# Filling TensorE's planned gaps with constant matmuls before the feed-forward part, and a plan in which the loads begin later

## The chip, the cores and the metric

The kernel runs on one core of one Trainium2 chip. The metric is the device time of one execution in microseconds; less is better. Three runs of the kernel before gave 295.18, 295.59 and 295.64 us, a median of 295.59 us.

## The reference

Two stages, one after the other, on 8 batches of 8 heads, 576 positions and head size 64. First a Nyströmformer attention, with 32 landmarks a head:

```python
q_lm = q.reshape(B, H, m, S // m, D).mean(axis=3)       # m = 32 landmarks
k_lm = k.reshape(B, H, m, S // m, D).mean(axis=3)
A = sm(q, k_lm); Bm = sm(q_lm, k_lm); C = sm(q_lm, k)    # scaled softmaxes
Z = Bm.T / (norm1(Bm) * norminf(Bm) + 1e-6)
for _ in range(6):
    Z = 2 * Z - Z @ Bm @ Z
attn = A @ Z @ C @ v
```

Then a feed-forward part on the 4608 positions of width 512, with a hidden width of 2048:

```python
h = attn_as_rows @ w_in            # 4608 x 512 @ 512 x 2048
g = maximum(h, 0) ** 2
out = g @ w_out                    # 4608 x 2048 @ 2048 x 512, float32
```

## The kernel before

All inputs come in float32 and are turned into bf16 by the loading DMAs, which GpSimd (POOL) issues: one for the k, q and v of each batch (`kb`, `qb`, `vb`), four for `w_in`, four for `w_out`. An issue waits until the load eight places earlier has landed (`LOADS = 8`). Stores go out from SP.

For each batch, `attention(b)` makes: the landmark means of k and q (`means`, into `mps`, matmuls with the constant `seg`, L334), scaled by `part` and turned by `folded` into the landmarks `lm` (L356); transposes of k and q on TensorE (`tps`, L458), evacuated to `kT` and `qT`; the small scores (`scores_b`, L379), whose normalised result is `bn`, with its column sums (`sums_b`, L406); the scores of q's landmarks against k (`scores_c`, `cps`, L490) with their maximum `nmc` and exponential `ec`; six steps of the iteration (`start_r` for `rps`, then `product` for `ips`, both L572, each followed by an update of `st` on VectorE); the transposes of `ec` (`turn_c`, `ctp`, L530) and the product with v (`times_v`, `ups`, L543), giving `u`; the scores of q (`scores_a`, `aps`, L700), for the first batch with the shift added by a matmul with `ident` (`shift_a`, L727); and the transposes of the normalised q scores (`transpose_a`, `atp`, L770) into `AT`. `times_z` (L631) gives `wT`, and `times_w_in` (L649) multiplies it with `w_in` into `G`, so that the first feed-forward matmul is G times AT.

The feed-forward part takes the positions in 9 stretches of 512. `ff_first` makes one 128x512 block of the hidden layer in the PSUM tag "h" (two buffers; `hps`, two matmuls or more, L848), ScalarE takes the relu (L855), VectorE the square (L860). `ff_second` makes 128 rows of the output from 16 matmuls (`ops`, L879).

The order of the instructions on each engine is made by the planner `Order`. Every step is added with an engine (or a choice of engines), a cost in us, the keys it reads and writes, and an urgency. `run` keeps in `free` the time at which each engine is through with what it was given, and in `end` the time at which each step ends. Again and again it works out for every step that could go next when it could start: not before its engine is free, not before its inputs' ends plus a latency (0.25 us after TensorE, 2.2 us after a DMA, 0.1 us else), and not before a PSUM slot is free. It takes the one that can start first, then the more urgent. Steps of batch 0 are kept by the length of the chain behind them. The step's `emit` is called at once, so instructions stand on every engine in the order in which the planner took them. No planned time is written into the program; engines run as soon as their semaphores allow. In this planner's terms a load is an issue of 0.8 us on POOL and a transfer of 3.05 us (k, q, v) or 2.5 us (weights).

Of the kernel before, what the change touches and what calls it, by code (L numbers as in the profile page):

```python
# [8 lines left out]
P = 128  # L9
# [5 lines left out]
BF16 = mybir.dt.bfloat16  # L15
F32 = mybir.dt.float32
# [14 lines left out]
SB = 512  # L31
# [28 lines left out]
class Order:  # L60
# [3 lines left out]

    BIAS = {"DVE": 0.6}
    LATENCY = {"PE": 0.25, "DMA": 2.2, "XBAR": 0.1, "SP": 2.5}

    def __init__(self, psum):  # L70
        self.slots = {tag: [0.0] * n for tag, n in psum.items()}
        self.tasks, self.writers, self.readers, self.taker = [], {}, {}, {}
        self.first, self.firsts = False, []

    def add(self, engine, cost, emit, reads=(), writes=(), urgency=0, takes=None, gives=None,
            reuses=()):

        i = len(self.tasks)
        deps = set()
        for key in list(reads) + list(writes):  # L80
            deps.update(self.writers.get(key, ()))
        for key in reuses:
            old = self.readers.get(key, []) + self.writers.get(key, [])
            deps.update(old)
            if gives is not None:

                self.tasks[self.taker[gives]][3].update(old)
        for key in reads:
            self.readers.setdefault(key, []).append(i)
        for key in writes:  # L90
            self.writers.setdefault(key, []).append(i)
        if takes:
            self.taker[takes[2]] = i
        self.tasks.append((engine, cost, emit, deps, urgency, takes, gives))
        if self.first:
            self.firsts.append(i)
        return i
# [30 lines left out]
        return seen  # L128

    def run(self):  # L130
        free, end, ran, held, left = {}, {}, {}, {}, list(range(len(self.tasks)))
        order, tail = [], self.tails()
        while left:
            best, other = None, None
            soon = self.coming(end, ran, free) if any(i not in end for i in self.firsts) else {}
            for i in left:
                choice, cost, _, deps, urgency, takes, _ = self.tasks[i]
                if any(d not in end for d in deps):
                    continue
                options = []  # L140
                for engine, cost in choice.items() if cost is None else ((choice, cost),):
                    start = free.get(engine, 0.0)
                    for d in deps:
                        start = max(start, end[d] + (self.LATENCY.get(ran[d], 0.1)
                                                     if ran[d] != engine else 0.0))
                    if takes:
                        at = sorted(self.slots[takes[0]])[:takes[1]]
                        if len(at) < takes[1]:
                            continue
                        start = max(start, at[-1])  # L150
                    options.append((start + cost + self.BIAS.get(engine, 0.0), start, engine, cost))
                for _, start, engine, cost in sorted(options)[:1]:
                    this = (start, urgency - tail.get(i, 0.0), i, cost, engine)
                    if other is None or this < other:
                        other = this
                    mine = tail.get(i, 0.0)
                    if any(e == engine and j != i and
                           max(at + tail[j], (at + c + mine) if mine else 0.0)
                           < max(max(at, start + cost) + tail[j], start + mine) - 0.05
                           for j, (e, at, c) in soon.items()):  # L160
                        continue
                    if best is None or this < best:
                        best = this
            start, _, i, cost, engine = best or other
            choice, fixed, emit, _, _, takes, gives = self.tasks[i]
            ran[i] = engine
            end[i] = free[engine] = start + cost
            if takes:
                slots = self.slots[takes[0]]
                slots.sort()  # L170
                del slots[:takes[1]]
                held[takes[2]] = [takes[0], takes[1], takes[3], 0.0]
            if gives is not None:
                h = held[gives]
                h[2] -= 1
                h[3] = max(h[3], end[i] + 0.1)
                if h[2] == 0:
                    self.slots[h[0]] += [h[3]] * h[1]
            left.remove(i)
            order.append((start, i))  # L180
            if emit is not None:
                if fixed is None:
                    emit(engine)
                else:
                    emit()
        self.ran = ran
        return order, end
# [3 lines left out]
def kernel(  # L191
# [9 lines left out]
    nc = tc.nc  # L201

    const = ctx.enter_context(tc.tile_pool(name="const", bufs=1))
# [4 lines left out]
    psum = ctx.enter_context(tc.tile_pool(name="psum", bufs=1, space=bass.MemoryType.PSUM))  # L208
# [9 lines left out]
    od = Order({"at": 2, "n": 1, "h": 2, "o": 1})  # L218
# [19 lines left out]
    def load(src, name, b, bufs):  # L238
        def go():
            t = T[name, b] = qkv.tile([TP, H, J * D], BF16, tag=name, bufs=bufs,  # L240
                                      name=f"{name}{b}")
            nc.gpsimd.dma_start(t[:], src[b].rearrange("h (p j) d -> p h (j d)", j=J))  # L242
        add_load(3.05, go, (name, b), -200 + b, [(name, b - bufs)])
# [20 lines left out]
    seg = const.tile([TP, M], BF16, name="seg")  # L264
    ones = const.tile([P, M], F32, name="ones")
    mask = const.tile([P, NPAIR], F32, name="mask")


    fold = const.tile([P, 3, P], BF16, name="fold")
# [12 lines left out]
                                compare_op=ALU.is_ge, fill=0.0, base=M - 1, channel_multiplier=-1)  # L282

    def fills():
        nc.vector.memset(seg_f[:], 1.0)
        nc.vector.memset(ones[:], 1.0)
        nc.vector.memset(mask[:], 1.0)
# [4 lines left out]
    def make_fold():  # L292
        nc.vector.memset(fold[:, 0:2], 0.0)
        for i in range(2):
# [3 lines left out]
                                    in0=fold[:, i, 64 * i:64 * i + 64], scalar1=0.125,  # L298
                                    scalar2=None, op0=ALU.mult)

    od.add("DVE", 1.0, fills, writes=["fills"], urgency=-20)
    load(k, "kb", 0, 2)
    load(q, "qb", 0, 2)
# [531 lines left out]
    def ff_first(s, f, at):  # L835
        segs, n = [], s * SB
        while n < (s + 1) * SB:
            b = n // S
            e = min((s + 1) * SB, (b + 1) * S)
            segs.append((b, n - b * S, e - b * S, n - s * SB))  # L840
            n = e
        box = {}

        def product():
            box["h"] = hps = psum.tile([P, SB], F32, tag="h", bufs=2, name=f"hps{s}")
            for b, lo, hi, o in segs:
                for g in range(2):
                    nc.tensor.matmul(hps[:, o:o + hi - lo],  # L848
                                     lhsT=T["G", b][:, g, P * f:P * f + P],
                                     rhs=T["AT", b][:, g, lo:hi],  # L850
                                     start=(g == 0), stop=(g == 1))

        def relu():
            box["r"] = r = moep.tile([P, SB], BF16, tag="r", bufs=5, name=f"r{s}")
            nc.scalar.activation(r[:], box["h"][:], AF.Relu)  # L855

        def square():
            if f == 0:
                T["gT", s] = moep.tile([P, NF, SB], BF16, tag="gT", name=f"gT{s}")
            nc.vector.tensor_tensor(T["gT", s][:, f, :], box["r"][:], box["r"][:], ALU.mult)  # L860

        u = at
        od.add("PE", 0.45, product, [key for b, lo, hi, _ in segs
                               for key in [("G", b, f // 4, 0), ("G", b, f // 4, 1)]
                               + [("AT", b, 0)] * (lo < 512) + [("AT", b, 1)] * (hi > 512)],
               [("hp", s, f)], u, takes=("h", 1, ("hps", s, f), 1))
        od.add("ACT", 0.6, relu, [("hp", s, f)], [("r", s * NF + f)], u, gives=("hps", s, f),
               reuses=[("r", s * NF + f - 5)])
        od.add("DVE", 0.45, square, [("r", s * NF + f)], [("gT", s, f)], u,
               reuses=[("gT", s - 2, i) for i in range(NF)])  # L870
# [37 lines left out]
    def feed(s):  # L908

        for i in range(NF):  # L910
            if s < N_SB:
                ff_first(s, i, 100 * s + 3 * i)
            if s:
                ff_second(s - 1, i // 4, 4 * (i % 4), 100 * s + 3 * i + 2)
# [44 lines left out]
```

## Time and profile before

| | |
|---|---|
| median of 3 runs | 295.59 us |
| the profiled execution's own time | 295.65 us |
| its span, first to last instruction | 293.9 us |
| TensorE (PE) busy | 268.2 us, 91% |
| weight loads (PEld) busy | 147.9 us |
| ScalarE (ACT) / VectorE (DVE) / GpSimd (POOL) busy | 180.7 / 171.5 / 28.1 us |
| mean granted TensorE clock | 0.985 |
| first PE instruction with data | 7.43 us |
| first `hps` matmul (L848) | 32.77 us |

The profile gives, for each engine, the time in which it ran an instruction, the granted TensorE clock as a share of full speed, the idle time before an instruction and what ended it ("issue" where the profile shows nothing that it waited for), and the chain of waits that ended last.

### The profile page before, as it was taken

Reading aid. Unit: us, or ns where it says so; the run is one execution under the profiler, and the core shown is the slowest. Engines: PE = TensorE matmul, PEld = TensorE weight load, DVE = VectorE, ACT = ScalarE, POOL = GpSimd, SP = SyncE. Lnnn points to the kernel's source line nnn. Section 1 sums busy time; section 2 is a strip of 40 time slices with the busy share of each in tenths; the row PEclk is TensorE's granted clock in tenths of the full one; section 3 lists DMA queues with packets and bytes.
Section 4 is the critical chain, followed back from the end, with each engine's and each line's share of the span. In section 5 each row is a group of like instructions: output and inputs, shape, how many; then the busy total and the mean of one; then the engine's idle time right before and its main releaser. Section 6 shows DMA issues by size and latency. Waiting matters only on the chain.

```text
span 293.9 us, 8012 instructions
## 1 busy us (share of the span) xinstructions
PE 268.2 (91%) x3357; PEld 147.9 (50%) x3403; DVE 171.5 (58%) x435; ACT 180.7 (61%) x334; POOL 28.1 (10%) x43
## 2 busy tenths in 40 slices
PE   0966889899999999999999999999999999999993
PEld 0744544555455555555656654565554444444441
DVE  1178499678849954986598368847775333323100
ACT  1447689676787847684777485566667745556220
POOL 8523212210030003000300000000000000000000
PEclk9999599999999999999999999999999999999998
DMA  7999999999999985992799201111111112211222
GB/s 97 204 205 207 205 206 203 204 218 129 186 165 217 162 167 79 216 197 59 112 198 175 52 21 37 39 38 38 36 39 38 45 49 53 71 38 38 67 74 71
DMA packets 52452, 34.20 MB, mean 116 GB/s; under 512 B 25280, under 2 KB 47808, under 8 KB 52416
## 3 DMA queue, kind: packets, MB, share of 16 engines
q0 software_dynamic: 23040, 18.35, 41.3%
q1 hardware_dynamic: 29376, 15.34, 26.4%
q8 instruction: 26, 0.43, 0.6%
q14 instruction: 10, 0.08, 0.1%
HBM read 36.70 MB, written 9.44 MB: 157 GB/s over the span
## 4 chain that ended last, share of the span: by engine, by line
PE 78%; DVE 9%; DMA 4%; ACT 3%; issue 3%; SPq 1%; POOL 0%; POOLq 0%
PE ops L879 38%; PE hps L848 21%; PE mps L334 3%; DMA qb<-in_q_dram 3%; PE gps L649 3%; PE ips L572 2%; PE ctp L530 2%; PE aps L700 2%; DVE G L224 2%; DMA out_dram<-o 1%; DVE gT L860 1%; PE atp L770 1%; ACT G L222 1%; DVE rsa L746 1%; PE cps L490 1%
## 5 line engine op out<-in xcount | busy, mean ns | idle before, releaser
L879 PE MATMUL ops<-w_out,gT 128*128 128x512 bf16 x534 | 137.9, 379 | 2.9 <-issue 1.1
L855 ACT ACTIVATE r<-hps 128x512 bf16<-128x512 f32 x144 | 83.2, 601 | 50.2 <-PE hps L848 47.4
L860 DVE TENSOR_TENSOR gT<-r 128x512 bf16<-128x512 bf16 x144 | 59.1, 428 | 44.9 <-ACT r L855 43.9
L848 PE MATMUL hps<-AT,G 128*128 128x512 bf16 (+7 forms) x508 | 82.7, 288 | 0.9 <-ACT r L855 0.3
L879 PEld LDWEIGHTS <-gT 128*128 128x128 bf16 x576 | 52.0, 98 | 50.2 <-issue 2.2
L848 PEld LDWEIGHTS <-G 128*128 128x128 bf16 x512 | 40.6, 98 | 27.7 <-issue 4.3
L224 DVE CAST G<-gps 128x512 bf16<-128x512 f32 x25 | 16.6, 688 | 22.3 <-ACT G L222 22.2
L222 ACT COPY o<-ops 128x512 f32<-128x512 f32 x31 | 18.2, 586 | 17.2 <-PE ops L879 11.2
L222 ACT CAST G<-gps 128x512 bf16<-128x512 f32 x39 | 21.3, 593 | 3.7 <-PE gps L649 3.2
L607 DVE SCALAR_TENSOR_TENSOR st<-st,ips 128x128 bf16<-128x128 bf16 x40 | 11.2, 280 | 7.6 <-PE ips L572 7.3
L507 ACT ACTIVATE ec<-cps,nmc 128x576 bf16<-128x576 f32 x16 | 11.7, 740 | 4.2 <-DVE nmc L498 4.2
L572 PEld LDWEIGHTS <-st 32*32 32x32 bf16 x384 | 5.6, 90 | 17.0 <-issue 5.0
L242 POOL DMA_DIRECT2D kb<-in_k_dram x8 | 6.4, 797 | 81.4 <-PE mps L334 76.5
L649 PE MATMUL gps<-w_in,wT 64*32 64x512 bf16 x256 | 12.5, 404 | 0.9 <-ACT wT L222 0.4
L572 PE MATMUL ips<-st 32*32 32x64 bf16 (+1 forms) x384 | 11.5, 194 | 1.9 <-DVE st L581 1.3
L334 PE MATMUL mps<-seg,kb 96*128 96x32 bf16 x192 | 6.1, 178 | 7.4 <-DMA kb<-in_k_dram 7.4
L222 ACT COPY ct<-ctp 96x1536 bf16<-96x1536 bf16 x7 | 10.0, 1435 | 3.8 <-PE ctp L530 3.7
L498 DVE TENSOR_REDUCE nmc<-cps 128x1 f32<-128x576 f32 x16 | 11.6, 750 | 0.8 <-PE cps L490 0.7
L746 DVE TENSOR_REDUCE rsa<-ea 128x36 f32<-128x1152 f32 (+2 forms) x10 | 11.1, 1106 | 0.4 <-ACT ea L736 0.2
L222 ACT COPY kT<-tps 128x1152 bf16<-128x1152 bf16 x6 | 6.7, 1128 | 7.5 <-PE tps L458 7.5
L712 DVE TENSOR_REDUCE ma<-aps 128x32 f32<-128x1024 f32 (+1 forms) x9 | 9.9, 1098 | 1.8 <-PE aps L700 1.1
L222 ACT COPY AT<-atp 128x1024 bf16<-128x1024 bf16 (+1 forms) x8 | 7.7, 959 | 4.5 <-PE atp L770 4.2
(89 smaller groups left out, 236.1 us busy)
## 6 DMA issues: line engine op xcount, KB each, us to landing
out_dram<-o SPq DMA_DIRECT2D x40, 128.0 KB, 2.4
kb<-in_k_dram POOLq DMA_DIRECT2D x8, 576.0 KB, 10.5
qb<-in_q_dram POOLq DMA_DIRECT2D x8, 576.0 KB, 13.2
vb<-in_v_dram POOLq DMA_DIRECT2D x8, 576.0 KB, 14.8
out_dram<-o SPq DMA_DIRECT2D x40, 64.0 KB, 1.9
w_in<-in_moe_w_in_dram POOLq DMA_DIRECT2D x4, 512.0 KB, 18.4
w_out<-in_moe_w_out_dram POOLq DMA_DIRECT2D x4, 512.0 KB, 21.0
out_dram<-o SPq DMA_DIRECT2D x8, 192.0 KB, 2.2
```

The costliest lines, as they stand in the source:

```text
L222: nc.scalar.copy(dst, src)
L224: nc.vector.tensor_copy(dst, src)
L334: nc.tensor.matmul(X["mps"][:, ti, h, :], lhsT=T[name, b][:, h, P * c:P * c + P], rhs=seg[:], start=(c == 0), stop=(c == 2))
L498: nc.vector.reduce_max(X["nmc"][:, g:g + 1], X["cps"][g][:, :, 0:HALF], axis=AX.XY, negate=True)
L507: nc.scalar.activation(X["ec"][:, g, :].rearrange("p (f n) -> p f n", f=2), X["cps"][g][:, :, 0:HALF], AF.Exp, bias=X["nmc"][:, g:g + 1], ...
L572: nc.tensor.matmul(out(r, g), lhsT=lhsT(r, g), rhs=rhs(r, g), start=True, stop=True)
L649: nc.tensor.matmul(gps[M * p:M * p + M, g, :], lhsT=X["wT"][r, p, :], rhs=w_in_bf[c][r, p, :], start=True, stop=True)
L746: nc.vector.reduce_sum(X["rsa"][:, r], X["ea"][:, r], axis=AX.X)
L848: nc.tensor.matmul(hps[:, o:o + hi - lo], lhsT=T["G", b][:, g, P * f:P * f + P], rhs=T["AT", b][:, g, lo:hi], start=(g == 0), stop=(g == 1))
L855: nc.scalar.activation(r[:], box["h"][:], AF.Relu)
L860: nc.vector.tensor_tensor(T["gT", s][:, f, :], box["r"][:], box["r"][:], ALU.mult)
L879: nc.tensor.matmul(T["o", s, ts][:], lhsT=T["gT", s][:, f, P * ts:P * ts + P], rhs=w_out_bf[f // 4][:, f % 4, :], start=(f == 0), stop=(f ...
```

## The change

Three things are added; nothing is taken away.

First, the planner starts with POOL free at 1.4 us instead of 0, so in the plan the loads begin 1.4 us later.

Second, DVE's first instruction becomes a memset of a 128x512 bf16 tile `plain` with ones, ahead of the three memsets that it did before.

Third, while the planner takes steps, up to the first `ff_first` product, it looks before each TensorE step at the planned idle time of TensorE in front of it. If that is over 0.3 us, `filler` is called first. It puts matmuls of `plain` with itself onto TensorE's queue, 512 columns at most each, down to 64, into a tile `dummy` that takes one of the two buffers of tag "h" and that nothing reads. The first call gives (gap - 1.0) x 1200 columns, each later one (gap - 0.2) x 2400, gap in us.

```diff
+    START = 1.4
     BIAS = {"DVE": 0.6}
...
+        self.filler, self.fill_until = None, None
...
-        free, end, ran, held, left = {}, {}, {}, {}, list(range(len(self.tasks)))
+        free, end, ran, held, left = {"POOL": self.START}, {}, {}, {}, list(range(len(self.tasks)))
...
             choice, fixed, emit, _, _, takes, gives = self.tasks[i]
+            if i == self.fill_until:
+                self.filler = None
+            if engine == "PE" and self.filler and start - free.get("PE", 0.0) > 0.3:
+                self.filler(start - free.get("PE", 0.0))
...
+    plain = const.tile([P, SB], BF16, name="plain")
...
     def fills():
+        nc.vector.memset(plain[:], 1.0)
         nc.vector.memset(seg_f[:], 1.0)
...
+    box = {}
+
+    def filler(time):
+        if "dummy" not in box:
+            box["dummy"] = psum.tile([P, SB], F32, tag="h", bufs=2, name="dummy")
+            columns = int((time - 1.0) * 1200)
+        else:
+            columns = int((time - 0.2) * 2400)
+        while columns >= 64:
+            n = min(columns, SB)
+            nc.tensor.matmul(box["dummy"][:, 0:n], lhsT=plain[:, 0:P], rhs=plain[:, 0:n],
+                             start=True, stop=True)
+            columns -= n
+
+    od.filler = filler
...
-        od.add("PE", 0.45, product, [key for b, lo, hi, _ in segs
+        ff = od.add("PE", 0.45, product, [key for b, lo, hi, _ in segs
...
+        if od.fill_until is None:
+            od.fill_until = ff
```

## The prediction

> **What bounds the kernel now.** I read the page's head and busy slices first, then the windows, then the start by the timeline, the chain of waits and POOL's rows, because every added matmul lies ahead of the first `hps` at 32.77 us.
>
> ```profile
> span 293.9 us, 8012 instructions
> PE   0966889899999999999999999999999999999993
> PEclk9999599999999999999999999999999999999998
> ```
>
> ```profile
> 30.00:32.00 2.00, 1.74 (x21) 1.07 (x17) 1.02 (x2) 0.72 (x2) 0.77 (x1) 0.50 1.30 203
> 40.00:50.00 10.00, 9.32 (x163) 5.12 (x166) 9.55 (x23) 9.59 (x17) 0.69 (x1) 1.00 1.30 204
> 150.00:200.00 50.00, 48.93 (x695) 28.52 (x704) 34.45 (x87) 33.56 (x63) 0.00 (x0) 1.00 0.36 70
> ```
>
> A window's columns are length, busy time of PE, PEld, DVE, ACT and POOL, granted clock, DMA share, GB/s. From 75 us on PE is full; from 40 to 50 us DVE and ACT are nearly full too. Whatever brings the start forward moves all this forward unchanged, so a microsecond won before the first `hps` should be one at the end. Loads keep the DMA queues at some 205 GB/s for the first 50 us and could cap that.
>
> ```profile
> 7.43 0.82 PE L334 MATMUL mps<-seg,kb 96*128 96x32 bf16 x24 [7.43 <-DMA kb<-in_k_dram]
> 8.09 2.08 PE L458 MATMUL tps<-ident,kb 96*128 96x96 bf16 x24
> ...
> 21.81 0.61 PE L727 MATMUL aps<-ma,ident 128*128 128x512 bf16 x1
> ...
> 23.21 0.38 PE L727 MATMUL aps<-ma,ident 128*128 128x512 bf16 x1 [0.56 <-DVE ma L712]
> ...
> 24.32 1.20 PE L458 MATMUL tps<-ident,kb 96*128 96x96 bf16 x24
> ...
> 29.57 0.48 PE L334 MATMUL mps<-seg,qb 96*128 96x32 bf16 x12 [1.39 <-issue]
> ...
> 34.47 1.04 PE L848 MATMUL hps<-AT,G 128*128 128x512 bf16 x2
> ```
>
> The same 24 transposes take 2.08 us at 8.09 and 1.20 at 24.32, the same L727 matmul 0.61 and 0.38. So PE runs at half rate until about 22.5 us, although the clock column says 1.00 there (nothing was recorded before the first change). It runs at full rate until 29.3 us and again at 0.50 until 36.1. PE was 95% busy from 7.4 to 14.0 without winning the clock: with transposes and 32-column matmuls. From 32.77 on, with 512-column ones, it won it in 3.4 us. That is the case for wide filler.
>
> **The plan.** Adding the planner's own costs: the first load is issued by 0.8 and its data usable at 0.8 + 0.1 + 3.05 + 2.2 = 6.15 us. Every TensorE step hangs on a load, so START moves the whole plan by 1.4 and the gaps stay; of the order only ties broken by rounding could change, which I price at nothing, with up to 0.3 us either way in the range. The first gap is 7.55 us: (7.55 - 1.0) x 1200 = 7860 columns, 16 matmuls. The planned gaps over 0.3 behind it: `mq` 1.35, `lps` 0.43, second `qb` transposes 0.34, `scores_b` 0.31, `scores_c` 1.32, `rps` 1.80, first `ips` 0.85, second 0.476, second `shift_a` 0.54, `times_z` 0.39, first `gps` 0.63, the two `atp` 0.33 and 0.79, `lps` of batch 1 0.55. Less 0.2 each, times 2400: 2760, 552, 336, 264, 2688, 3840, 1560, 662, 816, 456, 1032, 312, 1416, 840, in all 17,534 columns in 39 matmuls. The last 63 `ops` of 512 columns take 13.98 us, 0.22 each; so the later filler is 7.5 us at full rate and 15 at half.
>
> **First filler.** It waits for the memset of `plain` (a 96x32 f32 memset takes 0.09 us, 128x128 uint32 0.17; extrapolated 0.2 to 0.5), so it begins near 1.4 us. Behind it on PE wait only the means of `kb`, whose data come at 7.43. The three memsets that it delays are needed by POOL at 3.89: free by over 2 us. At half rate 7860 columns are 6.7 us, to 8.1; with the clock granted at w, the end is about (w + 8.0)/2. The 3.4 us that the row at 32.77 needed, up to twice that if the count starts at fixed times, put w at 4.8 to 8.2, so PE is 1 us early or 0.6 late; I take 0.1 late. `dummy` takes an `h` buffer, but its only users are earlier on PE's own queue: nothing, or one relu (0.60, L855).
>
> **To `scores_b`.** Transposes of `kb` 1.20 for 2.08: PE free at 9.3 instead of 10.17; filler 1.2, so the means of q start at 10.5 instead of 10.28 (a loss of 0.2: q lands at 10.24). Then full-rate rows: 12 transposes 0.60 for 0.97, `lps` 0.49 for 0.80; `bps` follows `lm` at 13.4 instead of the transposes at 14.04. Gain 0.65.
>
> **To `ips`.** The `scores_c` filler (1.2) ends at 14.8; `bn` is at 15.05 for 15.65 and `csp` ends at 15.75. The `rps` filler, 1.65, stands where the trace has 0.7 us: `rps` ends at 17.65 for 17.1. What covers it is the second `nmc` on DVE, which ends at 17.65 too and is ahead of `rps`'s reader; without it 0.5 is lost. The next filler (0.67) leaves the first `ips` at 18.3 for 18.41. So most of the 0.65 is eaten: gain 0.1.
>
> **To `gps`.** `ctp` 0.67 (the batch 1 row) for 1.30; two `aps` groups 0.3 for 0.54; L727 0.22 for 0.44. Sum 1.33, then 0.2 more off `ips` and waits: `ea`, `u`, `wT` follow 1.7 earlier; the `gps` filler ends 0.1 behind `wT`. The first `gps` starts at 25.15 for 26.77. Gain 1.6.
>
> **The stall and the second half-rate stretch.** At 28.18 PE stands 1.39 us inside a run of independent matmuls, on "issue". The page's DMA part has:
>
> ```profile
> q8 instruction: 26, 0.43, 0.6%
> ```
>
> The columns are packets, MB and share. That is 16 KB or 256 instructions a packet for PE's 6760; the stall looks like a late block of code among the loads. The filler adds 110 PE instructions (each matmul with its weight load), so the block's edge comes some 92 instructions earlier in the work, at about `wps`. There PE has waits anyway, but the block is asked for no sooner in time. Ends: all gone, -1.4, or the same again, 0; of the 26 blocks this is the only one where the waits list has an "issue" wait of a matmul over 0.2, which speaks for the gain, but it falls into the busiest stretch; I take half, -0.7. First `hps` then at 30.3 for 32.77: the fillers for `atp` and `lps` (0.13, 0.6, 0.36) eat 0.6 and full-rate `atp` 0.61 for 1.01, `gps` 0.41 for 0.63, `lps` 0.49 for 0.82 give 0.8. Sum here: -0.9.
>
> From 32.77 to 36.1 `gps` 0.62 for 1.06, two `hps` 0.59 for 1.04, `tps` 1.20 for 1.84, another `hps` 0.39 for 0.63: 1.77 us of PE time, partly under ACT's four copies of G. ACT's waits for `gps` there are 0.33 and 0.75. I take 0.6, between 0 and 1.77.
>
> **The DMA cap.** Of POOL's issues that wait for landings, the one at 30.47 waited for the last `w_in`, that at 36.16 for a `w_out`; the last `gps` (33.9) and first `ops` (41.65) could go 3.4 and 5 us earlier. No cap below 3.4.
>
> **Sum.** 0.1 late start (covered by q's landing: 0), -1.6, -0.9, -0.6: -3.1. On the profiled 295.65 this gives 292.55; the median lies 0.06 below. I say 292.5. With the stall gone and all of 1.77: -5.0, 290.7. With the stall whole and no gain behind it: -1.8, 293.8.
>
> [...] The clock windows show changes at 29.3 and 36.1, 6.8 us apart. [...]
>
> **Rivals.** (1) *The clock comes late* (slower). If the grant isn't there when the `mq` filler starts at about 9.3 to 10.2, that filler takes 2.4 us: +2.2. Then `scores_c`'s takes 2.4 and `rps`'s 3.3 in place of 0.7, so `rps` is up to 5.8 late. Less the 1.6 to 3 won afterwards: about +2, 297.5. For: 95% busy did not win the clock at 7.4 to 14. Against: 6 us of 512-column work did what 3.4 did at 32.77. It decides if no grant comes by 10.2. 10%.
> (2) *The clock falls again* behind the first filler, as at 29.3. For: PE was busy 1.5 of each 2 us from 24 to 28 and still lost it, so what holds the clock is not known. Against: wide work now stands in nearly every gap. If it falls: half the gain and doubled filler, 294.6. 17%.
> (3) *It does nothing*: `rps`, the code stall and the `atp` fillers each end 0.6 to 1 later, so the overshoot eats the clock: 295.6. 8%.
>
> **How the numbers follow.** My forecast (290.7 to 293.8) holds 65%, (2) 17%, (3) 8%, (1) 10%. Range: 290.7 to 295.2, which leaves out (1), half of (3) and some edges. A measurement of this kernel can tell 0.2%, 0.6 us, from no change. Forecast and (2), with a little of (3): faster 0.83; same 0.06; slower 0.11.
>
> **What would show it.** Right: `tps` at 8 us takes 1.2; L727 0.38 both times; `ctp` of batch 0 0.7 to 0.8; no 0.50 window before 40 us; first `hps` at 29.5 to 31; PE's 75 to 280 us unchanged but shifted. The stall should appear elsewhere, before 28 us, or shrink. Wrong: filler matmuls of 0.43 us behind 9 us, `rps` ending later than 17.7, or a first `hps` at 32 or later.

## The result and the profile after

The changed kernel takes 294.6 us (median of 10 runs, 293.62 to 294.89) against 295.6 (10 runs, 295.15 to 295.95): a ratio of 0.996, 95% interval 0.9946 to 0.9974. It is faster by 1.0 us. The prediction had 292.5, a gain of 3.1, so the direction was right and two thirds of the gain did not come. The time lies inside the range of 290.7 to 295.2. The profiled execution has a span of 293.0 us, 0.9 less than before.

The page's head, with the busy slices and the granted clock:

```profile
span 293.0 us, 8118 instructions
...
PE   7999797999999999999999999999999999999993
...
PEclk9999997999999999999999999999999999999999
```

106 more instructions are recorded, PE is busy from the first slice, and the stretch at half clock has moved from the fifth slice (29.3 to 36.2 us) to the seventh (46.7 to 50.1 us) and is half as long. Times at which the clock changes, here and below, are those of the trace's clock record. The timeline of PE up to 50 us, in columns start, busy time, instruction and, in brackets, the idle time before it:

```profile
1.52 5.55 PE L322 MATMUL dummy<-plain 128*128 128x512 bf16 x16 [1.52 <-DVE seg_f L294]
7.46 0.77 PE L360 MATMUL mps<-seg,kb 96*128 96x32 bf16 x24 [0.39 <-DMA kb<-in_k_dram]
8.08 1.18 PE L484 MATMUL tps<-ident,kb 96*128 96x96 bf16 x24
...
17.09 0.22 PE L598 MATMUL rps<-bnT 32*32 32x32 bf16 x8
...
20.24 0.38 PE L753 MATMUL aps<-ma,ident 128*128 128x512 bf16 x1
...
26.18 0.75 PE L360 MATMUL mps<-seg,qb 96*128 96x32 bf16 x24
...
29.24 0.59 PE L874 MATMUL hps<-AT,G 128*128 128x512 bf16 x2
...
46.31 0.84 PE L484 MATMUL tps<-ident,kb 96*128 96x96 bf16 x12 [1.82 <-DMA kb<-in_k_dram]
```

Up to the first `hps` the gain is larger than predicted: the `kb` transposes take 1.18 us for 2.08, L727 (now L753) 0.38 for 0.61, the 24 means of q run through without the 1.39 us stall, and the first `hps` starts at 29.24, where 30.3 was forecast and the kernel before had 32.77. That is a lead of 3.5 us. The last line is the new wait: the transposes of batch 2's k stand 1.82 us for the load of that k. Before, the timeline had them at

```profile
47.80 0.68 PE L458 MATMUL tps<-ident,kb 96*128 96x96 bf16 x12
```

with no wait. In the chain of waits of the kernel after, between 40 and 56 us, the load is the link:

```profile
25.66 20.61 DMA kb<-in_k_dram
46.27 0.05 issue
46.31 0.84 PE tps L484 x12
```

The load is issued at 25.66 (25.59 before) and needs 20.6 us, since k, q, v of two batches and all weights go ahead of it in a queue that moves at the same rate (205 GB/s from 10 to 26 us and 206 from 26 to 46, in both kernels). It landed at 46.27 us here and at 46.07 in the kernel before, although TensorE was 3.5 us ahead: the load caps the lead. Its first use before was at 47.80, so of the 3.5 us, 1.5 are left there. Then, behind the idle stretch, the clock falls, as the windows show (length; busy time of PE, PEld, DVE, ACT, POOL; clock; DMA share; GB/s):

```profile
44.40:46.30 1.90, 0.09 (x1) 0.00 (x0) 1.90 (x4) 1.43 (x3) 0.00 (x0) 1.00 1.30 198
46.80:50.00 3.20, 2.98 (x62) 1.86 (x61) 2.10 (x4) 1.94 (x3) 1.75 (x2) 0.50 1.31 205
```

For 3.4 us PE runs at half rate, and at 50.31 the next four `ops` matmuls begin where they began before, at 50.30: nothing is left of the lead. The 0.9 us that the span does gain come back at `wps`, which before waited 0.90 us for DVE's `zt`; DVE had kept part of its lead. Before:

```profile
50.30 1.03 PE L879 MATMUL ops<-w_out,gT 128*128 128x512 bf16 x4
...
53.42 0.30 PE L631 MATMUL wps<-zt,u 128*64 128x32 bf16 x8 [0.90 <-DVE zt L613]
```

After:

```profile
50.31 1.03 PE L907 MATMUL ops<-w_out,gT 128*128 128x512 bf16 x4
...
52.47 0.30 PE L657 MATMUL wps<-zt,u 128*64 128x32 bf16 x8
```

One of the ten runs has a mean clock of 0.999, which leaves no room for a half-rate stretch of 3.4 us. It took 293.73 us, so the wait costs time without the fall too.

### The profile page after: what moved, and what is told of

Same layout as the page of the kernel before. It is cut to its first block, busy times and chain, and to the rows that moved or that the text cites. A ratio compares the mean times of both kernels' runs of the same rounds, so it can differ in the third digit from the quotient of the medians.

```text
span 293.0 us, 8118 instructions
## 1 busy us (share of the span) xinstructions
PE 276.0 (94%) x3407; PEld 149.1 (51%) x3458; DVE 172.9 (59%) x436; ACT 181.2 (62%) x334; POOL 28.1 (10%) x43
## 4 chain that ended last, share of the span: by engine, by line
PE 75%; DMA 14%; DVE 3%; ACT 2%; POOL 2%; issue 2%; SPq 1%; POOLq 0%
PE ops L907 38%; PE hps L874 21%; DMA kb<-in_k_dram 7%; DMA w_in<-in_moe_w_in_dram 6%; PE mps L360 2%; PE ips L598 2%; PE gps L675 2%; PE ctp L556 2%; DMA out_dram<-o 1%; DVE G L231 1%; PE atp L796 1%; PE ups L569 1%; PE aps L726 1%; PE tps L484 1%; ACT part L370 1%
## 5 line engine op out<-in xcount | busy, mean ns | idle before, releaser
L886 DVE TENSOR_TENSOR gT<-r 128x512 bf16<-128x512 bf16 x144 | 59.9, 434 | 44.8 <-ACT r L881 43.8
L229 ACT COPY o<-ops 128x512 f32<-128x512 f32 x31 | 18.1, 585 | 17.2 <-PE ops L907 11.2
L322 PE MATMUL dummy<-plain 128*128 128x512 bf16 (+12 forms) x49 | 13.9, 406 | 2.3 <-DVE seg_f L294 1.5
## 6 DMA issues: line engine op xcount, KB each, us to landing
w_out<-in_moe_w_out_dram POOLq DMA_DIRECT2D x4, 512.0 KB, 20.6
```

The lines of the kernel that those rows point to most:

```text
L229: nc.scalar.copy(dst, src)
L322: nc.tensor.matmul(box["dummy"][:, 0:n], lhsT=plain[:, 0:P], rhs=plain[:, 0:n], start=True, stop=True)
```

## The experiments

Each run is compared with runs of the kernel before on the same chip.

**Fewer loads, with and without filler.** Three of the four `w_out` loads are left out, and all four chunks use the one tile that is loaded:

```diff
 def go():
+    if any(t is not None for t in w_out_bf):
+        w_out_bf[c] = [t for t in w_out_bf if t is not None][0]
+        return
     w_out_bf[c] = const.tile([P, 4, D_MODEL], BF16, name=f"w_out{c}")
```

With the filler:

> The changed kernel, but only one of the four w_out loads is made and all four chunks use that tile (three quarters of w_out are left out). Three loads of 0.52 MB fewer stand ahead of batch 2's k, so by the load rate of 205 GB/s (2.6 us each in the trace) it lands near 38.5 instead of 46.3 us. Theory (the loads cap the gain): the wait of 1.8 us at 46.3 and the half-rate stretch behind it vanish, first hps stays at 29.2, and the time falls to 291.5 to 292.5, 3 to 4 below the kernel before. Rival (the gain is lost between 40 and 50 us where VectorE and ScalarE are nearly full, the load only being the last to arrive): 293.8 to 294.6, as the changed kernel.

Measured 292.92 us, ratio 0.992 (0.9897 to 0.9943). That is 0.4 above the 291.5 to 292.5 of the theory and 0.9 below the rival's range. In its trace the transposes of batch 2's k start at 44.70 without a wait, and the clock stays granted from 5.4 to 288.7 us. The control without filler:

> The kernel before with only one of the four w_out loads (three quarters of w_out left out), the control. Theory (loads cap only what starts early): batch 2's k was used at 47.8 and landed about 46.3, so nothing waits for it and the time stays at 295.2 to 295.8. Rival (fewer loads help by themselves, by a code block that comes sooner or by freer memory): 294 or less; the 1.4 us stall at 28.2 lies ahead of the point where the loads differ in landing, so it should stay.

Measured 295.94 us, ratio 1.0011 (1.0002 to 1.002). So with the loads out of the way the filler is worth some 3 us, and the loads alone nothing: the theory that loads cap the lead holds, and the rival that the lead is lost among busy engines between 40 and 50 us falls. One expectation missed. In the control's profiled execution the stall near 28 us is gone, and the clock is granted only at 34.7 us, so TensorE comes to that place at half rate (0.83 us for the 24 means, where the run with the first filler alone has 0.75 at full rate):

```profile
28.88 0.83 PE L337 MATMUL mps<-seg,qb 96*128 96x32 bf16 x24
```

**The same by order alone.** All work kept; the loads of POOL in another order:

```diff
-            if b > 1:
+            if b > 2:
                 load(k, "kb", b, 2)
                 load(q, "qb", b, 2)
-            if b:
+            if b > 1:
                 load(v, "vb", b, 3)
             if b == 1:
-                for c in range(4):
-                    load_w_out(c)
+                load_w_out(0)
+                load(v, "vb", 1, 3)
+                load_w_out(1)
+                load(k, "kb", 2, 2)
+                load(q, "qb", 2, 2)
+                load_w_out(2)
+                load_w_out(3)
```

> The changed kernel with only POOL's order of loads changed: after the w_in loads come w_out 0, k of batch 2, v of batch 1, w_out 1, q of batch 2, w_out 2, w_out 3. All work is kept, and the order on the other engines is the same. Batch 2's k should land near 36 to 37 us, v of batch 1 near 39.5, q of batch 2 near 45, the last w_out near 50. Theory (the loads cap the gain): 291.5 to 292.6, no TensorE wait for a load after 10 us, no half clock at 46.7. Rival (lost elsewhere between 40 and 50): 293.8 to 294.6. A third way: v of batch 1 or w_out 1 becomes the late one, 293 to 294, with a wait on that load in the trace.

Measured 292.31 us, ratio 0.9891 (0.9877 to 0.9904). PE waits for no load over 0.3 us after 8 us, and batch 2's k is there when its transposes come:

```profile
44.43 0.68 PE L484 MATMUL tps<-ident,kb 96*128 96x96 bf16 x12
```

The control:

> The kernel before with the same reordered loads, the control: nothing waited for batch 2's k there, so theory says 295.3 to 295.8, no change. Rival (the order of loads helps by itself): 294.5 or less.

Measured 295.75 us, ratio 1.0006 (0.9997 to 1.0015): no difference. The 3.4 us lead at these transposes (44.43 for 47.80) is still there at the end, in a span of 290.6 for 293.9.

**One load alone.** Only batch 2's k moved ahead of the last `w_out` load:

```diff
             if b == 1:
-                for c in range(4):
+                for c in range(3):
                     load_w_out(c)
+                load(k, "kb", 2, 2)
+                load_w_out(3)
```

The loop no longer loads k for b = 2.

> The changed kernel with one swap on POOL: batch 2's k is loaded ahead of the last w_out load instead of behind it. Theory (that one k load is the cap): it lands one w_out load earlier, 2.6 us, near 43.7, ahead of its first use at 44.4; batch 2's q still lands near 49.2 where its transposes could start at 48.5, a wait of 0.7 that the 0.9 wait for zt behind it covers; 292.2 to 292.9. Rival (the whole queue of loads is late, q and v as much as k): the wait moves to q of batch 2 and 293.3 to 294.6.

Measured 292.42 us, ratio 0.9892 (0.9875 to 0.9908). The wait does move to q, but it is short and `wps` waits less for `zt` in turn:

```profile
44.67 0.68 PE L484 MATMUL tps<-ident,kb 96*128 96x96 bf16 x12
...
49.29 0.68 PE L484 MATMUL tps<-ident,qb 96*128 96x96 bf16 x12 [0.41 <-DMA qb<-in_q_dram]
50.29 0.30 PE L657 MATMUL wps<-zt,u 128*64 128x32 bf16 x8 [0.31 <-DVE zt L639]
```

One swap of two loads gives back 2.2 of the missing 2.3 us (292.42 for 294.6; 292.31 with all loads reordered). That settles the cause.

**Which filler matters** (with reordered loads, so that the cap hides nothing). Only the first filler (the later ones `return` at once):

> Reordered loads, and only the first filler (16 matmuls before batch 0's k); the 39 later ones are left out. If the early clock alone makes the gain and the later filler only keeps it: the clock comes near 5 us, and without later filler it falls again once, somewhere between 12 and 29 us, for 6.8 us; 293 to 294.5. If the later filler mainly costs (it overshoots the real waits) and the clock stays without it: 291.6 to 292.2, below the 292.3 with all filler.

Measured 294.99 us, 294.04 to 296.27 in 10 runs, ratio 0.9983 (0.9966 to 1.0), so above the range expected and no clear gain. In the profiled execution the clock comes at 4.64 us and falls twice, not once:

```profile
15.00:21.00 6.00, 3.97 (x70) 3.05 (x70) 4.18 (x15) 2.52 (x6) 1.54 (x2) 0.50 1.28 204
...
29.00:31.00 2.00, 1.88 (x13) 0.69 (x12) 0.69 (x1) 1.69 (x3) 0.79 (x1) 0.50 1.25 208
```

Only the later filler:

> Reordered loads, and only the later fillers; TensorE waits idle for the first load as in the kernel before. Theory (a late clock doubles the filler): the fillers for the means of q, the k scores and rps run at half rate until some wide filler has won the clock, near 12 to 16 us; the first hps at 30.5 to 32.5 and 293 to 295. Rival (the first filler is not needed, the 1.2 us filler at 10 us wins the clock as well): 292.3 to 292.8.

Measured 295.21 us, ratio 0.9976 (0.9959 to 0.9992), 0.2 above the range expected. The filler for the means of q runs at half rate and pushes them to 12.23 us, 1.8 later than with all filler and the same loads (10.45):

```profile
10.18 2.21 PE L322 MATMUL dummy<-plain 128*128 128x512 bf16 x6
12.23 0.76 PE L360 MATMUL mps<-seg,qb 96*128 96x32 bf16 x24
```

The two parts alone give 0.7 us, which the interval does not tell from nothing, and 0.4; together they give 3.3. The first wins the clock (at 4.64 us with it alone); with the later ones no fall came behind it (mean clock 0.996 with all filler and reordered loads, 0.98 with the first alone); and without the first, the filler ahead of the grant at 11.97 us is paid at half rate (2.21 us for the six matmuls above).

**How much is needed.** Half of the columns of each later filler, `int((time - 0.2) * 1200)`, with reordered loads:

> Reordered loads and the first filler whole; each later filler has half its columns. If the later filler overshoots the real waits (the rps filler ends at 17.1 where its inputs are there by 16.3) but is needed to hold the clock only in part: 291.8 to 292.2. If half of it no longer holds the clock: a 0.50 window between 12 and 32 us and 293 to 295, with a spread of over 1 us between runs, as with the first filler alone (294.0 to 296.3).

Measured 291.68 us, 291.63 to 291.74, ratio 0.9868 (0.9853 to 0.9883): by the ratio 3.9 us under the kernel before, and the fastest of all. The overshoot, filler that outlasts the wait it fills, was worth 0.6. With a quarter (`* 600`):

> Reordered loads, the first filler whole, each later filler with a quarter of its columns. If only the overshoot counts: a little below half filler, 291.3 to 291.7. If the clock needs more than that: a 0.50 window between 12 and 32 us in some executions, 292.5 to 295 and a spread of over 1 us.

Measured 294.17 us, 293.11 to 294.65, ratio 0.9935 (0.9911 to 0.9959). In the windows of its profiled execution the clock is lost from 17.2 to 30.9 us:

```profile
20.00:24.00 4.00, 3.73 (x96) 1.98 (x95) 2.36 (x7) 2.52 (x3) 1.52 (x2) 0.50 1.24 206
24.00:28.00 4.00, 3.96 (x67) 3.04 (x67) 3.81 (x12) 1.91 (x4) 0.89 (x2) 0.50 1.24 206
```

Half filler in the old order of loads:

> The changed kernel with the loads in their old order and each later filler halved. If batch 2's k load is the cap, TensorE only comes to it earlier and waits longer: the 0.6 us that half filler wins with reordered loads (292.31 to 291.68) is not seen, 293.6 to 294.9 as the changed kernel, and the wait at 46.3 grows from 1.8 to some 2.4 us. If overshoot were what ate the gain: 293.0 to 293.6.

Measured 294.77 us, ratio 0.9946 (0.9927 to 0.9965): capped as expected. The wait at 46.4 did not grow, though; the lead had already been spent on other loads, of `w_in` (the first `hps` here is at 28.60) and `w_out`:

```profile
31.02 0.41 PE L675 MATMUL gps<-w_in,wT 64*32 64x512 bf16 x8 [0.95 <-DMA w_in<-in_moe_w_in_dram]
...
38.34 1.02 PE L907 MATMUL ops<-w_out,gT 128*128 128x512 bf16 x3 [0.33 <-DMA w_out<-in_moe_w_out_dram]
...
46.41 0.68 PE L484 MATMUL tps<-ident,kb 96*128 96x96 bf16 x12 [1.76 <-DMA kb<-in_k_dram]
```

**The stall and the clock.** Reordered loads, 55 matmuls of 64 columns in the first gap, and no other filler:

```diff
-            columns = int((time - 1.0) * 1200)
+            columns = 55 * 64
         else:
-            columns = int((time - 0.2) * 2400)
+            return
         while columns >= 64:
-            n = min(columns, SB)
+            n = min(columns, 64)
```

> Reordered loads; the filler is replaced by 55 matmuls of 64 columns, all in the first idle stretch, 110 instructions as with the full filler, done before batch 0's k lands. If the stall of 1.4 us at 28 us is a late code block, moving its edge by 110 instructions takes it away or to a place with a wait: no issue wait of a matmul over 0.4 us near 28, time 294 to 294.8. If the stall belongs to that place in the work (data or a semaphore): it stays and the time is 295.3 to 295.8. Small matmuls may win some clock; the trace tells, and half-rate rows up to 22 us are expected.

Measured 295.69 us, ratio 0.9991 (0.9973 to 1.0009). The stall is gone, all 24 means of q run through at 28.90, but in this execution the clock is never granted before 36.8 us, and L753 takes 0.58 at 23.22 where the kernel before had 0.38:

```profile
23.22 0.58 PE L753 MATMUL aps<-ma,ident 128*128 128x512 bf16 x1 [0.56 <-DVE ma L738]
...
28.90 0.80 PE L360 MATMUL mps<-seg,qb 96*128 96x32 bf16 x24
```

So the expectation on the stall held and that on the time did not: in this execution, what the stall gave, the missing full-rate stretch took. But the run does not show that the stall went because code moved. The control with fewer `w_out` loads moves no instruction of PE, has its clock late too (34.7), and runs through the same means at 28.88. A cleaner case is the run with the first filler alone, 32 instructions of PE (16 matmuls with their weight loads). There the clock is at full rate from 21.7 to 28.5 us, as in the kernel before from 22.5 to 29.3, and there is no stall:

```profile
26.77 0.75 PE L360 MATMUL mps<-seg,qb 96*128 96x32 bf16 x24
```

Last, the first gap filled with 32-column matmuls, and no other filler:

```diff
-            columns = int((time - 0.2) * 2400)
+            return
...
-            n = min(columns, SB)
+            n = 32
...
-            columns -= n
+            columns -= 40
```

> Reordered loads; only the first gap is filled, with 197 matmuls of 32 columns in place of 16 of 512. TensorE is then as busy as with the wide ones. If the clock is won by busy time, it comes near 5 us as with the wide filler; if by columns streamed, as the half rate from 7.4 to 14 us of the kernel before suggests, it does not come before 15 us, and the k transposes at 8 us take 2.1 us, not 1.2. Its time is disturbed by 394 more instructions and is not compared.

The clock came at 5.08 us, so the reading that narrow matmuls cannot win it is refuted; it was lost again at 8.49, until 35.8. And with 394 more instructions the stall turned up in the middle of batch 0's k transposes:

```profile
8.19 0.33 PE L484 MATMUL tps<-ident,kb 96*128 96x96 bf16 x4
9.57 1.76 PE L484 MATMUL tps<-ident,kb 96*128 96x96 bf16 x20 [1.05 <-issue]
```

The trace has 447 matmuls and weight loads ahead of this stall, and 701 ahead of the one at 28.18 in the kernel before. The two differ by 254. The prediction put 256 instructions into one packet of the queue `q8`; by the pages it is 260 in the kernel before (6760 matmuls and weight loads, 26 packets) and 254 in the kernel after (6865, 27 packets), which is an estimate, since no row says which instructions a packet holds. In both, a packet of `q8` is moved just ahead of the stall: from 6.99 to 7.88 us here, from 27.14 to 28.10 before.

The one time of this run, 296.44 us, is not compared.

## Why the prediction was wrong, step by step

*The step that failed is "The DMA cap".* It looked at two landings, the last `w_in` and a `w_out`, found that their users could go 3.4 and 5 us earlier, and said "No cap below 3.4". It left out the loads of batch 2. When they land could be worked out from rows that it had. The issue at 30.47 had waited for the last `w_in`. Behind that come v of batch 1, four `w_out` loads and k of batch 2, and the waits of POOL show one landing every 2.5 to 2.9 us, the longer for the 0.59 MB of a k, q or v. Twice 2.9 and four times 2.5 make 46.3 as an estimate; the trace after has 46.27. The first use of that k is not its means (54.98 us) but the transposes at 47.80. The slack was 1.5 us, less than half of the lead.

*The sum without a cap* was 292.5, and the run with one load swapped gave 292.42. Part of that agreement is luck. The terms up to `gps` held (1.6 predicted, 1.5 measured). From there to the first `hps` 0.9 was predicted and 2.0 came; 0.7 of the difference is the stall's. The 0.6 behind the first `hps` did not come at all: the lead is 3.5 us at 32.77 and still 3.5 where `ops` starts (38.18 for 41.65). That the measured 294.6 is the very number of rival 2 is luck too: its mechanism, a fall at the planned gaps and filler at half rate, is not what the trace shows.

*The rule that a lead ahead of `hps` is a lead at the end* held, where no load was in the way: 3.4 us at 44 us, 3.3 at the end, with reordered loads. DVE and ACT, busy 95% and 96% between 40 and 50 us before, did not eat it.

*The first filler*: begin 1.52 (1.4 predicted), end 7.07, 0.39 ahead of the load. The grant came at 5.72, inside 4.8 to 8.2. That a count may start at fixed times was the author's assumption; the grant came 4.2 us behind the filler's begin here, and 3.1 behind it in the run with the first filler alone (1.53 to 4.64). The memset took 0.48 us (0.2 to 0.5) and held nothing up. The later start of the loads in the plan is part of every run with filler and was not tested by itself.

*To `scores_b`* 0.8 us were won (`bps` at 13.17 for 13.96) for 0.65. *To `ips`*: `rps` started at 17.09 and its reader on DVE at 17.46, as the cover by the second `nmc` said; the first `ips` came at 18.00 for 18.41, a gain of 0.4, not 0.1. *To `gps`*: 25.23 predicted at 25.15, 1.5 us.

*The stall* was set at half, -0.7; it was all gone in every kernel with full filler. As a term it was mis-sized on the careful side. The counts of 701 and 447 speak for the edge of a block of code, which would move with the number of instructions ahead of it; no run shows such an edge as such. It was not felt in the control at half rate, which began these means at 28.88, where the kernel before began them at 27.73. That the blocks arrive late because the loads fill the queues is argued, not tested.

*The half-rate stretch* from 29.3 to 36.2 vanished as forecast, but another of 3.4 us appeared at 46.7 behind the new wait. In the profiled executions with all filler or half of it and the load out of the way there was none.

*Rival 1*, the late clock, is what the later filler without the first shows: the `mq` filler took 2.21 us (2.4 said). But the clock came at 11.97, soon enough that the kernel was not slower: 295.21, not 297.5. *Rival 2*, a clock that falls again, happened, by a load and not by the planned gaps. *Rival 3* had the overshoot: half filler showed it to be 0.6 us.

*The size of the gain, and the clock.* With half filler and reordered loads 3.9 us were won, 1.3%. Up to 1.4 us of that is the stall's, and the 2.5 that are left are 0.9%. Among the stretches of the clock's record are 3.41, 6.83, 10.24 and 13.65 us, one to four times 3.41: half clock for 3.41 us in the changed kernel (46.7 to 50.1) and for 6.83 in the kernel before (29.3 to 36.2), full clock for 10.24 with the first filler alone, half clock for 13.65 with a quarter of the later filler (17.2 to 30.9). An idle stretch of 1.8 us from 44.5 came just before the fall at 46.7, the stall of 1.39 us from 28.18 before that at 29.3.

## What to carry to other kernels

Before counting on a lead, list for every load its landing and the first instruction of any kind that reads it; the smallest difference caps the lead. Here the queue was full (205 GB/s), and the landing moved by 0.2 us while its user came 3.5 us earlier. With filler meant to hold TensorE's clock, test its parts and its amount each by itself: here the two parts alone gave 0.7 and 0.4 us and together 3.3, with a grant at 5.72 us where the first part was in and at 11.97 where it was not; half of the later part was better than the whole (291.68 for 292.31), and with a quarter the clock was lost from 17.2 to 30.9 us (294.17). Where the granted clock differs between executions of one kernel (means of 0.957 to 0.98 in 10 runs with the first filler alone, 0.996 to 0.999 in 4 runs with all filler and reordered loads), compare spreads as well as medians: 294.04 to 296.27 in the one, 292.29 to 292.33 in the other.

## What the runs showed of the hardware

32-column matmuls with a weight load each won the clock in 3.6 us (195 of them, some 130 by the grant at 5.08) when nothing stood between them, though 24 means, 24 transposes, 24 means and 12 transposes from 7.4 to 12 us did not in the kernel before, whose first change of the clock is at 22.5; which of these instructions made the difference was not tested.

With only the later filler the clock fell from 35.9 to 39.3 us although PE had been busy 21.1 of the 23 us from 12 to 35. The last 3.41 us before the fall look different from those ahead of them: 2.05 us busy, 60%.

```profile
12.00:35.00 23.00, 21.13 (x417) 13.08 (x416) 15.26 (x43) 14.42 (x30) 6.19 (x8) 1.00 1.27 205
36.00:39.00 3.00, 3.00 (x37) 0.84 (x30) 2.71 (x9) 1.67 (x4) 0.77 (x1) 0.50 1.28 207
```

The same count with columns for PE alone (length; busy time; clock; DMA share; GB/s):

```profile
25.60:29.00 3.40, 2.99 (x74) 1.00 1.25 205
29.00:32.45 3.45, 3.15 (x47) 1.00 1.26 206
32.45:35.86 3.41, 2.05 (x47) 1.00 1.31 203
```

So it goes in all profiled executions, when the first 60 us are cut into such stretches from the clock's first change on. The nine falls came behind stretches that were busy 47% to 77%, and every stretch at full clock below 61% had a fall behind it. Above that and up to 77% the clock fell behind three and held behind others, so the share of busy time alone does not tell these apart. The stretch before the fall at 46.7 in the changed kernel was busy 47%, that before the fall at 29.3 in the kernel before 50%.
